# Regrouping the steps at the border of two mixture layers: each block's turn placed in steps of the other block

## The chip, the cores and the metric

The kernel runs on one core of a Trainium2 chip. The metric is the device time of one execution in microseconds (us), smaller being better. The core has five engines that run side by side, each through its own list of instructions in a fixed order: TensorE (PE in the rows, with PEld for its weight loads), VectorE (DVE), ScalarE (ACT), GpSimd (POOL) and SyncE (SP), which here issues the DMA transfers. An engine whose next instruction must wait holds back everything behind it in its list.

## The reference

Block attention gives a matrix x of 1536 rows and 512 columns, and two mixture-of-experts layers follow. The first has 4 experts and given weights, the second 8 experts and weights from a gate on its own input.

```python
def _moe_ref(x, domain_probs, w1, w2):          # first layer, E = 4
    p = domain_probs / (domain_probs.sum(-1, keepdims=True) + 1e-09)
    for e in range(E):
        h = np.maximum(x @ w1[e], 0.0)          # (1536, 1024)
        out += p[:, e:e + 1] * (h @ w2[e])      # (1536, 512)
...
def _moe2_ref(x, w_gate, w1, w2):               # second layer, E = 8
    logits = x @ w_gate
    P = np.exp(logits - logits.max())
    for _ in range(8):                          # rows, then columns
        P /= P.sum(1, keepdims=True) + 1e-09
        P /= P.sum(0, keepdims=True) + 1e-09
        P *= N / E
    for e in range(E):
        out += P[:, e:e + 1] * (np.maximum(x @ w1[e], 0.0) @ w2[e])
```

## The kernel before, in words

**Units, blocks, steps.** A unit is one expert's slice of 256 hidden columns: units 0 to 15 are the first layer, 16 to 47 the second. The rows of x are two blocks of 768. A step (u, b) is unit u on block b, 96 steps in all; before the change they go (0,0), (0,1), (1,0), (1,1) and so on.

**Two halves of a step.** Every fp32 factor is split into a high and a low part (names in hi and lo), and three matmuls stand for one. The first half of a step is seven products P1 to P7 of six matmuls each (`step_products`, L487), a fast block multiplication with seven products in place of eight. Its operands are sums and differences, made ahead for the weights (`w1_pieces`) and for x (`x_pieces`). P1, P3, P5 and P7 accumulate into one PSUM bank `px`, P2 and P6 into another (also named px in the rows), P4 into `pz`. Between them the bank must be read: ScalarE copies it after P1, P2 and P3 (c11 L521, c22 L526, c12 L530), VectorE adds it to c11 after P4, to c22 after P5, to c12 after P6 (L516). So P3 waits for the copy after P1, P5 for the copy after P3, and P7 for the addition to c22 after P5. ScalarE makes hhi from c by relu (L495) and VectorE makes hlo from both (L500). The second half is G: six tiles of six matmuls with w2 (`g2_tile`, L562 to L564), each followed by VectorE's accumulation into `acc` (L582). A step ordinarily runs its own seven products and then the G of the step before it.

**Weights.** SyncE loads w1 (L141) and w2 (L149) of a unit into `scr`, three buffers that serve in turn. ScalarE writes the high parts (L125), GpSimd the differences (L178) and the low parts (L128). `w1_pieces` and `w2_pieces` stand in the lists behind a step's products. Two sets of weights, a and b, alternate by unit.

**The turn.** When a block's first layer is done, its `acc` is transposed by TensorE (pxt, L592, eight groups of three), copied by ScalarE into two `scr` buffers (L596), and made into x operands. `x_pieces` has six rounds for each of two half-buffers, here r1 to r6: r1 casts 768 columns (ScalarE), low part by GpSimd; r2 casts 384 columns, low part by VectorE; r3 two subtractions on VectorE (L211); r4 casts their results, low part by GpSimd; r5 two more subtractions; r6 casts those, low part by VectorE. The gate (`gate_logits`: pg, gs, pl) and `sinkhorn` follow.

**Order.** `weave` takes a string, and each letter emits the next piece of one generator: P a product, G a tile, w a weight piece, T a turn piece, L a gate piece, s a piece of sinkhorn. This order is the order in every engine's list. At the border, block 0 is turned in step (15,1) by BND1 and BND2, and block 1 in step (16,0) by BND3 and BND4. In these two steps the products are followed by the step's own G.

Of the kernel before, what the change touches and what calls it, by code (L numbers as in the profile page):

```python
# [18 lines left out]
def local_global_attention_moe_moe(  # L19
# [13 lines left out]
    nc = tc.nc  # L33
# [162 lines left out]
    def w2_pieces(u, hi_eng, lo_eng):  # L196
        w = wsets[u % 2]
        s = stage[u, 2]
        for c in range(FC):
            yield split(w["w2hi"][:, c], w["w2lo"][:, c], s[:, c], hi_eng, lo_eng)  # L200
# [276 lines left out]
    def new_xf():  # L477
        return scratch(2, 2 * BLK)

    def product(u, b, a, x, pm, first=True):  # L480
        w = wsets[u % 2]
        n = 3 * KH
        i = 0
        for c in range(KH):
            xhi, xlo = xop[b, c]
            for l, r in (("w1hi", xhi), ("w1hi", xlo), ("w1lo", xhi)):
                nc.tensor.matmul(  # L487
                    pm, w[l][:, a, c, :], r[:, x, :],
                    start=first and i == 0, stop=i == n - 1, skip_group_check=True,
                )  # L490
                i += 1

    def relu_hi(u, b, f, t, c):
        hhi = hsets[(u * NB + b) % 2][0]
        nc.scalar.activation(out=hhi[:, f, t * HB:(t + 1) * HB], in_=c, func=AF.Relu)  # L495

    def relu_lo(u, b, f, t, c):
        hhi, hlo = hsets[(u * NB + b) % 2]
        sl = slice(t * HB, (t + 1) * HB)
        nc.vector.scalar_tensor_tensor(  # L500
            out=hlo[:, f, sl], in0=c, scalar=0.0, in1=hhi[:, f, sl].bitcast(F32),
            op0=ALU.max, op1=ALU.subtract,
        )

    def step_products(u, b):

        def temp(name):
            return xp.tile([P, HB], F32, name=name)  # L510

        def bank():
            return ps_x.tile([P, 512], F32, name="px", tag="x")[:, 0:HB]

        def add(c, pm):
            nc.vector.tensor_tensor(out=c, in0=pm, in1=c, op=ALU.add)  # L516

        px = bank()
        product(u, b, A11, B11, px)
        c11 = temp("c11")  # L520
        nc.scalar.copy(out=c11, in_=px)  # L521
        yield
        py = bank()
        product(u, b, S1, T1, py)
        c22 = temp("c22")
        nc.scalar.copy(out=c22, in_=py)  # L526
        yield
        product(u, b, S2, T2, px, False)
        c12 = temp("c12")
        nc.scalar.copy(out=c12, in_=px)  # L530
        yield
        pz = ps_m.tile([P, HB], F32, name="pz", tag="m")
        product(u, b, A12, B21, pz)
        add(c11, pz)
        relu_hi(u, b, 0, 0, c11)
        yield
        product(u, b, S3, T3, px, False)
        add(c22, px)
        relu_hi(u, b, 1, 1, c22)
        relu_lo(u, b, 0, 0, c11)  # L540
        yield
        product(u, b, S4, B22, py, False)
        add(c12, py)
        relu_hi(u, b, 0, 1, c12)
        relu_lo(u, b, 1, 1, c22)
        yield
        product(u, b, A22, T4, px, False)
        relu_hi(u, b, 1, 0, px)
        relu_lo(u, b, 0, 1, c12)
        relu_lo(u, b, 1, 0, px)  # L550
        yield

    raw, lg = set(), {}

    def g2_tile(u, b, t):
        layer, e, f = units[u]
        w = wsets[u % 2]
        hhi, hlo = hsets[(u * NB + b) % 2]
        pm = ps_m.tile([P, DM], F32, name="pm", tag="m")
        ts = slice(t * P, (t + 1) * P)  # L560
        for c in range(FC):
            nc.tensor.matmul(pm, hhi[:, c, ts], w["w2hi"][:, c, :], start=(c == 0), stop=False)  # L562
            nc.tensor.matmul(pm, hhi[:, c, ts], w["w2lo"][:, c, :], start=False, stop=False)  # L563
            nc.tensor.matmul(pm, hlo[:, c, ts], w["w2hi"][:, c, :], start=False, stop=(c == FC - 1))  # L564
        T = b * TPB + t
        first = e == 0 and f == 0
        if layer == 1 and "p" not in lg:
            assert e == 0
            raw.add(T)
            if first:  # L570
                nc.scalar.copy(out=acc[T], in_=pm)
            else:
                nc.vector.tensor_tensor(out=acc[T], in0=pm, in1=acc[T], op=ALU.add)
            return
        scal = (p1 if layer == 0 else pp)[:, T, e:e + 1]
        if T in raw:
            raw.remove(T)
            nc.vector.tensor_scalar_mul(acc[T], acc[T], pp[:, T, 0:1])
        if first:
            nc.vector.tensor_scalar_mul(acc[T], pm, scal)  # L580
        else:
            nc.vector.scalar_tensor_tensor(  # L582
                out=acc[T], in0=pm, scalar=scal, in1=acc[T], op0=ALU.mult, op1=ALU.add
            )
        if u == NU - 1:
            nc.sync.dma_start(out=out[T * P:(T + 1) * P, :], in_=acc[T])
# [11 lines left out]
    def turn_pieces(b):  # L598

        for c in range(KH):  # L600
            xfs[b, c] = new_xf()
            for th in range(2):
                for dh in range(2):
                    yield transpose_x(b, c, th, dh)
        los = (nc.gpsimd, nc.vector, nc.gpsimd, nc.vector)
        halves = [
            x_pieces(b, c, xfs[b, c], xfs[b, c], nc.scalar, los, nc.vector) for c in range(KH)
        ]
        for _ in range(6):
            for h in halves:  # L610
                yield next(h, None)

    def gate_logits(b):

# [57 lines left out]
        yield  # L672
        lg["p"] = pp

    def g2_tiles(u, b):
        for t in range(TPB):
            yield g2_tile(u, b, t)

    DONE = object()

# [8 lines left out]
    def head_of(gen, n):  # L689
        for _ in range(n):  # L690
            if next(gen, DONE) is DONE:
                return
            yield

    def chain(*gens):
        for g in gens:
            yield from g

    L = E1 * NFU - 1
    BND1, BN1 = "wwGGGGGGPTTTTPTPTTTPTPTPTPTTT", 15  # L700
    BND2 = "TGTGTGTGTGTG"
    BND3, BN3 = "PTPTTTPTPTTTPTPTPTTTT", 14
    BND4 = "TGTLGTLGTLGTLGTLGL"
    ENTRY = "GPwGPwGwPwGPwGPwGPwPww"
    STEADY = "PPPPPPPwGwGwGwGwwGwwG"
    LATE = "PsPsPsPsPsPsPwsGwsGwsGwwsGwwsGwsG"
    with tc.manual_schedule():
        early = chain(step_products(0, 0), g2_tiles(0, 0))
        side = {}

        def filler(w, n):
# [42 lines left out]
        with tc.tile_pool(name="attn", bufs=1) as apool:  # L754
# [13 lines left out]
        )  # L768
        weave(
            "PPwPwPwPwPwPw",  # L770
            P=step_products(0, 1),
            G=early,
            w=chain(
                w1_pieces(1, nc.vector, nc.gpsimd, nc.vector),
# [3 lines left out]
        load_w1(2)  # L778
        load_w2(2)

        def w_pieces(u, b):
            if u >= NU:
                return iter(())
            if b == 0:
                return w1_pieces(u, nc.scalar, nc.gpsimd, nc.gpsimd)
            return w2_pieces(u, nc.scalar, nc.gpsimd)

        for u in range(1, NU):
            for b in range(NB):
                prev = (u, 0) if b else (u - 1, 1)  # L790
                tiles = g2_tiles(*prev)
                prod = step_products(u, b)
                if (u, b) == (L, 1):
                    turn = turn_pieces(0)
                    weave(
                        BND1,
                        P=prod, G=tiles, T=head_of(turn, BN1), w=w_pieces(u + 1, 1),
                    )
                    weave(BND2, G=g2_tiles(u, 1), T=turn)
                elif (u, b) == (L + 1, 0):  # L800
                    turn = turn_pieces(1)
                    weave(BND3, P=prod, T=head_of(turn, BN3))
                    weave(BND4, G=g2_tiles(u, 0), L=gate_logits(0), T=turn)
                    load_w1(u + 1)
                    load_w2(u + 1)
                elif (u, b) == (L + 1, 1):
                    weave(
                        "wPLwPLwPLwPLwPLwPLwP", P=prod, L=gate_logits(1),
                        w=chain(w_pieces(u + 1, 0), w_pieces(u + 1, 1)),
                    )  # L810
                    load_w1(u + 2)
                    load_w2(u + 2)
                    sink = sinkhorn()
                else:
                    w = w_pieces(u + 1, b)
                    if u > L and "p" not in lg:
                        weave(
                            LATE, P=prod, G=tiles, w=w, s=head_of(sink, 12),
                        )
                    else:  # L820
                        order = ENTRY if (u, b) == (1, 0) else STEADY
                        weave(order, P=prod, G=tiles, w=w)
                    if u + 2 < NU and (u, b) != (L, 0):
                        (load_w2 if b else load_w1)(u + 2)
        for _ in g2_tiles(NU - 1, 1):
            pass


# [26 lines left out]
```

## Time and profile before

| what | value |
|---|---|
| time, median of 3 runs | 1644.41 us (1643.33 to 1644.82) |
| time of the profiled execution | 1645.07 us |
| its span, first to last instruction | 1643.4 us |
| TensorE busy | 1599.0 us, 97% of the span |
| VectorE, ScalarE, GpSimd busy | 56%, 36%, 34% |
| mean granted TensorE clock | 0.990 |
| stretch of the border, 600 to 664.56 us | TensorE busy 58.40 of 64.56 us |

Busy time is the time in which an engine ran an instruction; a matmul's row is longer than the distance to the next one's start, because matmuls overlap. The granted clock is 1.00 at 2.4 GHz and 0.50 at 1.2 GHz. What an engine waited for is told in brackets, with the instruction that released it.

### The profile page before, as it was taken

The numbers are of one execution on the slowest core, as the hardware profiler recorded it, in microseconds if no ns is written. First come the engines' busy times: TensorE is split into PE (matmuls) and PEld (weight loads), VectorE is DVE, ScalarE is ACT, GpSimd is POOL, SyncE is SP. The second block draws the span as 40 slices with busy tenths as digits, with TensorE's granted clock in tenths as the row PEclk, the third lists the DMA queues.
The fourth block names the chain that finished last, engine by engine and source line by source line (L and its number), as shares of the span: only waits on it lengthen the run. The fifth ranks groups of instructions, "written<-read, shape, count | busy, mean of one in ns | idle before, by whom it ended". The sixth has DMA issues, their size and how long they took to land.

```text
span 1643.4 us, 21876 instructions
## 1 busy us (share of the span) xinstructions
PE 1599.0 (97%) x8419; PEld 1437.7 (87%) x8419; DVE 922.3 (56%) x1711; ACT 586.5 (36%) x1369; POOL 558.3 (34%) x642
## 2 busy tenths in 40 slices
PE   6879999999999999999999999999999999999999
PEld 5768899899899987889998998998998999989987
DVE  6886554554554556675555555545545545555555
ACT  4763233333333335433333333323323323323321
POOL 3644333323324333424324324324323323333330
PEclk9889999999999999999999999999999999999999
DMA  9831001001001100101100100100100100100102
GB/s 185 161 83 52 26 26 52 27 26 50 28 26 40 38 1 26 53 26 41 37 27 31 47 26 27 52 26 27 52 27 27 51 26 26 52 26 26 52 0 78
DMA packets 84520, 70.26 MB, mean 43 GB/s; under 512 B 36032, under 2 KB 69056, under 8 KB 84416
## 3 DMA queue, kind: packets, MB, share of 16 engines
q1 hardware_dynamic: 84416, 68.87, 14.5%
q8 instruction: 66, 1.08, 0.3%
q14 instruction: 38, 0.31, 0.1%
HBM read 64.53 MB, written 3.15 MB: 41 GB/s over the span
## 4 chain that ended last, share of the span: by engine, by line
PE 90%; DVE 6%; ACT 1%; issue 1%; DMA 1%; POOL 0%; SPq 0%; DVEq 0%; ACTq 0%
PE px L487 35%; PE pm L564 16%; PE pm L563 16%; PE pm L562 16%; PE pz L487 6%; ACT s L398 1%; DVE scr L211 1%; DVE vr L342 1%; DVE s L388 1%; DVE sm L402 1%; PE pg L622 0%; DVE hlo_b L500 0%; DVE c L516 0%; DMA vn<-in_v_dram 0%; DMA scr<-in_moe_w_dram 0%
## 5 line engine op out<-in xcount | busy, mean ns | idle before, releaser
L582 DVE SCALAR_TENSOR_TENSOR acc<-pm,pp,acc 128x512 f32<-128x512 f32 x359 | 269.6, 751 | 195.0 <-PE pm L564 193.3
L516 DVE TENSOR_TENSOR c<-pz,c 128x384 f32<-128x384 f32 x96 | 53.4, 557 | 317.9 <-PE pz L487 317.8
L128 POOL TENSOR_TENSOR w1lo_b<-scr,w1hi_b 128x512 fp32r<-128x512 f32 (+1 forms) x144 | 116.9, 830 | 317.0 <-ACT w1hi_b L125 309.4
L128 POOL TENSOR_TENSOR w1lo_a<-scr,w1hi_a 128x512 fp32r<-128x512 f32 (+1 forms) x144 | 118.4, 841 | 305.9 <-ACT w1hi_a L125 296.0
L521 ACT COPY c<-px 128x384 f32<-128x384 f32 x96 | 46.1, 480 | 436.6 <-PE px L487 436.5
L487 PE MATMUL px<-xhi,w1hi_a 128*128 128x384 f32 x576 | 195.5, 339 | 2.0 <-ACT c L521 1.0
L487 PE MATMUL px<-xhi,w1hi_b 128*128 128x384 f32 x576 | 194.1, 337 | 0.8 <-ACT c L530 0.8
L487 PE MATMUL px<-xlo,w1hi_a 128*128 128x384 f32 x576 | 193.8, 336 | 0.2 <-POOL xlo L128 0.2
L487 PE MATMUL px<-xhi,w1lo_a 128*128 128x384 f32 x576 | 193.8, 336 | 0.0
L487 PE MATMUL px<-xhi,w1lo_b 128*128 128x384 f32 x576 | 193.3, 336 | 0.0
L487 PE MATMUL px<-xlo,w1hi_b 128*128 128x384 f32 x576 | 193.3, 336 | 0.0
L582 DVE SCALAR_TENSOR_TENSOR acc<-pm,p,acc 128x512 f32<-128x512 f32 x180 | 135.0, 751 | 97.0 <-PE pm L564 97.0
L178 POOL TENSOR_TENSOR scr<-scr 128x256 f32<-128x256 f32 x188 | 137.6, 742 | 3.7
L516 DVE TENSOR_TENSOR c<-px,c 128x384 f32<-128x384 f32 x192 | 107.0, 557 | 46.6 <-PE px L487 46.5
L128 POOL TENSOR_TENSOR w2lo_a<-scr,w2hi_a 128x512 fp32r<-128x512 f32 x48 | 61.2, 1296 | 161.8 <-ACT w2hi_a L125 159.1
L128 POOL TENSOR_TENSOR w2lo_b<-scr,w2hi_b 128x512 fp32r<-128x512 f32 x48 | 60.9, 1292 | 161.0 <-ACT w2hi_b L125 161.0
L564 PE MATMUL pm<-w2hi_b,hlo_b 128*128 128x512 f32 x288 | 113.4, 394 | 2.3 <-DVE hlo_b L500 2.3
L495 ACT ACTIVATE hhi_a<-c 128x384 fp32r<-128x384 f32 x144 | 75.6, 525 | 112.0 <-DVE c L516 112.0
L562 PE MATMUL pm<-w2hi_b,hhi_b 128*128 128x512 f32 x288 | 112.8, 391 | 0.5 <-ACT hhi_b L495 0.5
L562 PE MATMUL pm<-w2hi_a,hhi_a 128*128 128x512 f32 x288 | 112.5, 391 | 0.7 <-ACT hhi_a L495 0.7
L564 PE MATMUL pm<-w2hi_a,hlo_a 128*128 128x512 f32 x288 | 112.6, 391 | 0.5 <-DVE hlo_a L500 0.5
L495 ACT ACTIVATE hhi_b<-c 128x384 fp32r<-128x384 f32 x144 | 75.6, 525 | 104.6 <-DVE c L516 104.5
(148 smaller groups left out, 3613.0 us busy)
## 6 DMA issues: line engine op xcount, KB each, us to landing
scr<-in_moe_w_dram SPq DMA_DIRECT2D x96, 512.0 KB, 4.6
vs<-in_v_dram SPq DMA_DIRECT2D x16, 240.0 KB, 4.8
kn<-in_k_dram SPq DMA_DIRECT2D x16, 192.0 KB, 4.0
qn<-in_q_dram SPq DMA_DIRECT2D x16, 192.0 KB, 4.4
vn<-in_v_dram SPq DMA_DIRECT2D x8, 384.0 KB, 3.8
out_dram<-acc SPq DMA_DIRECT2D x12, 256.0 KB, 2.0
vs<-vb SPq DMA_DIRECT2D x8, 144.0 KB
vs<-in_v_dram SPq DMA_DIRECT2D x32, 24.0 KB, 4.5
```

Source lines behind the costliest of these rows:

```text
L128: lo_eng.tensor_tensor(out=lo, in0=src, in1=hi.bitcast(F32), op=ALU.subtract)
L178: sum_eng.tensor_tensor(out=st[:, o], in0=x, in1=y, op=op)
L211: sum_eng.tensor_tensor(out=out, in0=x, in1=y, op=ALU.subtract)
L342: nc.vector.tensor_reduce(out=vr[i], in_=vn[i].rearrange("x h c d -> x h d c"), axis=AX.X, op=ALU.add)
L487: nc.tensor.matmul(pm, w[l][:, a, c, :], r[:, x, :], start=first and i == 0, stop=i == n - 1, skip_group_check=True,)
L495: nc.scalar.activation(out=hhi[:, f, t * HB:(t + 1) * HB], in_=c, func=AF.Relu)
L516: nc.vector.tensor_tensor(out=c, in0=pm, in1=c, op=ALU.add)
L521: nc.scalar.copy(out=c11, in_=px)
L562: nc.tensor.matmul(pm, hhi[:, c, ts], w["w2hi"][:, c, :], start=(c == 0), stop=False)
L563: nc.tensor.matmul(pm, hhi[:, c, ts], w["w2lo"][:, c, :], start=False, stop=False)
L564: nc.tensor.matmul(pm, hlo[:, c, ts], w["w2hi"][:, c, :], start=False, stop=(c == FC - 1))
L582: nc.vector.scalar_tensor_tensor(out=acc[T], in0=pm, scalar=scal, in1=acc[T], op0=ALU.mult, op1=ALU.add)
```

## The change

Steps are now listed by number n in `steps`. Units 14 and 15 go as (14,0), (15,0), (14,1), (15,1), and units 16 and 17 as (16,0), (17,0), (16,1), (17,1); all other pairs keep their order. Block 0 is turned during (14,1) and (15,1), block 1 during (16,0) and (17,0), by the strings TURN1 and TURN2. The gate of block 0 stands in (16,1) and that of block 1 in (17,1) (GATE). Every step runs the G of the step before it, at the border too. The w1 pieces of a unit stand in the step just ahead of its first, its w2 pieces in its first step; before, they stood one unit earlier. `sinkhorn` begins at (18,0) in place of (17,0).

```diff
-        for u in range(1, NU):
-            for b in range(NB):
-                prev = (u, 0) if b else (u - 1, 1)
...
-    BND1, BN1 = "wwGGGGGGPTTTTPTPTTTPTPTPTPTTT", 15
-    BND2 = "TGTGTGTGTGTG"
-    BND3, BN3 = "PTPTTTPTPTTTPTPTPTTTT", 14
-    BND4 = "TGTLGTLGTLGTLGTLGL"
-    ENTRY = "GPwGPwGwPwGPwGPwGPwPww"
+        order += (a, c, x, y) if u in (L - 1, L + 1) else (a, x, c, y)
+    steps = [(u, b, n) for n, (u, b) in enumerate(order)]
...
+    w1_in = {first[u] - 1: u for u in range(2, NU)}
+    w2_in = {first[u]: u for u in range(2, NU)}
...
+        loads.setdefault(first[u] - 2, []).append((load_w1, u))
...
+        loads.setdefault(first[u] - 1, []).append((load_w2, u))
...
+    ENTRY = "GPGPGPwGwPGPwGPwGPwPww"
     STEADY = "PPPPPPPwGwGwGwGwwGwwG"
     LATE = "PsPsPsPsPsPsPwsGwsGwsGwwsGwwsGwsG"
+    TURN1 = "PPwGwGwGwGwGwGwwwwPTTPTTPTTPTTPT"
+    TURN2 = "PTPTPTPTPTPwPwGwGwGwGwGwGwww"
+    GATE = "PLPLPLPLPLPLPLGwLGwLGwLGwLGwG"
...
         for _ in range(6):
             for h in halves:
-                yield next(h, None)
+                next(h, None)
+            yield
...
+            if S[0:2] in ((L - 1, 1), (L + 1, 0)):
+                turn = turn_pieces(0 if S[1] else 1)
+                more, letters = {"T": head_of(turn, TURN1.count("T"))}, TURN1
+            elif S[0:2] in ((L, 1), (L + 2, 0)):
+                more, letters = {"T": turn}, TURN2
```

VectorE's list in step (15,1) before: c11, c22 and c12 are the three additions, xlo00 and xlo01 the low parts of block 0's two halves, and the rows at L211 are the subtractions of r3.

```order
L516 TENSOR_TENSOR c11_5365<-pz_5426,c11_5365 128x384
L516 TENSOR_TENSOR c22_5395<-px_5358,c22_5395 128x384
L500 SCALAR_TENSOR_TENSOR hlo_b_1609<-c11_5365,hhi_b_1608 128x384
L516 TENSOR_TENSOR c12_5409<-px_5388,c12_5409 128x384
L500 SCALAR_TENSOR_TENSOR hlo_b_1609<-c22_5395,hhi_b_1608 128x384
L128 TENSOR_TENSOR xlo00_82<-scr_5367,xhi00_81 128x384
L500 SCALAR_TENSOR_TENSOR hlo_b_1609<-c12_5409,hhi_b_1608 128x384
```

The same engine in step (15,1) of the changed kernel (its lines are numbered one or two higher), with r2, r3, r5 and r6 in order.

```order
L128 TENSOR_TENSOR xlo00_82<-scr_5249,xhi00_81 128x384
L128 TENSOR_TENSOR xlo01_84<-scr_5250,xhi01_83 128x384
L211 TENSOR_TENSOR scr_5249<-scr_5249 128x384 x2
L211 TENSOR_TENSOR scr_5250<-scr_5250 128x384 x2
L517 TENSOR_TENSOR c11_5340<-pz_5371,c11_5340 128x384
L211 TENSOR_TENSOR scr_5249<-scr_5249 128x384 x2
L211 TENSOR_TENSOR scr_5250<-scr_5250 128x384 x2
L517 TENSOR_TENSOR c22_5353<-px_5333,c22_5353 128x384
L501 SCALAR_TENSOR_TENSOR hlo_b_1609<-c11_5340,hhi_b_1608 128x384
L128 TENSOR_TENSOR xlo00_82<-scr_5249,xhi00_81 128x768
L128 TENSOR_TENSOR xlo01_84<-scr_5250,xhi01_83 128x768
L517 TENSOR_TENSOR c12_5365<-px_5346,c12_5365 128x384
```

Before, the three additions stood ahead of all subtractions; now two low parts and eight subtractions stand ahead of the addition to c22.

ScalarE's list in the same step of the changed kernel, from the last relu of the step before to the cast of r4: xhi00 and xhi01 are the casts, px_5333 and px_5346 the two banks of (15,1).

```order
L496 ACTIVATE hhi_a_97<-px_5175 128x384
L125 CAST xhi00_81<-scr_5249 128x768
L125 CAST xhi01_83<-scr_5250 128x768
L522 COPY c11_5340<-px_5333 128x384
L125 CAST xhi00_81<-scr_5249 128x384
L125 CAST xhi01_83<-scr_5250 128x384
L527 COPY c22_5353<-px_5346 128x384
L531 COPY c12_5365<-px_5333 128x384
L125 CAST xhi00_81<-scr_5249 128x768
```

Before, the step's first copy c11 stood ahead of all casts of the turn; now two casts of 768 columns stand between the last relu and that copy.

## Rows read from the trace of the kernel before

**Rows 1.** Stretches, TensorE alone: length, busy time and instructions, granted clock, DMA share, GB/s.
```profile
398.09:406.25 8.16, 8.16 (x37) 1.00 0.01 2
406.25:413.58 7.33, 7.33 (x43) 1.00 0.41 143
600.00:664.56 64.56, 58.40 (x315) 0.97 0.07 22
114.35:120.18 5.83, 5.77 (x46) 0.51 0.01 3
615.16:618.31 3.15, 3.15 (x7) 0.50 0.00 0
```

**Rows 2.** What TensorE waited for, whole span: us in total, times, longest.
```profile
PE pm L564 <- DVE hlo_b L500: 2.3, 1, 2.3
...
PE pl L634 <- ACT gs L628: 1.2, 2, 0.6
...
PE pxt L592 <- DVE acc L582: 0.9, 2, 0.5
PE px L487 <- ACT c L530: 0.8, 1, 0.8
PE pm L562 <- ACT hhi_a L495: 0.7, 1, 0.7
PE pm L562 <- ACT hhi_b L495: 0.5, 1, 0.5
PE pm L564 <- DVE hlo_a L500: 0.5, 1, 0.5
```

**Rows 3.** Timeline of TensorE in a step of sinkhorn: P6's last matmul, P7's first.
```profile
703.57 0.34 PE L487 MATMUL px<-xhi,w1lo_a 128*128 128x384 f32 x1
704.80 0.45 PE L487 MATMUL px<-xhi,w1hi_a 128*128 128x384 f32 x1 [0.89 <-DVE c L516]
```

**Rows 4.** Timeline of an ordinary step with w1 pieces, ScalarE: start us, us, instruction.
```profile
404.80 1.11 ACT L125 CAST w1hi_a<-scr 128x256 fp32r<-128x256 f32 x3 [1.93 <-POOL scr L178]
```

**Rows 5.** Timeline of the same step and the next, GpSimd.
```profile
399.33 1.29 POOL L128 TENSOR_TENSOR w1lo_a<-scr,w1hi_a 128x512 fp32r<-128x512 f32 x1 [13.00 <-ACT w1hi_a L125]
...
405.43 2.13 POOL L128 TENSOR_TENSOR w1lo_a<-scr,w1hi_a 128x256 fp32r<-128x256 f32 x3
414.86 2.54 POOL L128 TENSOR_TENSOR w2lo_a<-scr,w2hi_a 128x512 fp32r<-128x512 f32 x2 [7.30 <-ACT w2hi_a L125]
```

**Rows 6.** Timeline of ScalarE early on: a cast of x and the copy behind it.
```profile
132.44 0.83 ACT L125 CAST xhi<-scr 128x768 fp32r<-128x768 f32 x1 [2.40 <-DVE scr L211]
133.18 0.47 ACT L521 COPY c<-px 128x384 f32<-128x384 f32 x1
```

**Rows 7.** Timeline of the turn of block 0, VectorE.
```profile
612.00 2.17 DVE L128 TENSOR_TENSOR xlo<-scr,xhi 128x384 fp32r<-128x384 f32 x1
...
615.49 2.34 DVE L211 TENSOR_TENSOR scr<-scr 128x384 f32<-128x384 f32 x4
617.75 0.75 DVE L582 SCALAR_TENSOR_TENSOR acc<-pm,p,acc 128x512 f32<-128x512 f32 x1
618.41 3.65 DVE L211 TENSOR_TENSOR scr<-scr 128x384 f32<-128x384 f32 x2
...
622.64 1.01 DVE L211 TENSOR_TENSOR scr<-scr 128x384 f32<-128x384 f32 x2
624.24 0.94 DVE L128 TENSOR_TENSOR xlo<-scr,xhi 128x768 fp32r<-128x768 f32 x1
```

**Rows 8.** The same stretch, GpSimd.
```profile
609.81 3.94 POOL L128 TENSOR_TENSOR xlo<-scr,xhi 128x768 fp32r<-128x768 f32 x2 [13.37 <-ACT xhi L125]
617.64 4.00 POOL L128 TENSOR_TENSOR xlo<-scr,xhi 128x768 fp32r<-128x768 f32 x2 [3.89 <-ACT xhi L125]
```

**Rows 9.** Timeline of TensorE: four groups of transposes in a row.
```profile
601.84 1.47 PE L592 MATMUL pxt<-ident,acc 128*128 128x128 f32 x12
```

**Rows 10.** DMA of 620 to 700 us: weight loads, KB each, median us to landing.
```profile
scr<-in_moe_w_dram SPq DMA_DIRECT2D x6, 512.0 KB, 3.5
```

More of the change, by code (lines that the diff above doesn't have):

```diff
@@ L478, in new_xf, with product @@
         return scratch(2, 2 * BLK)
-    def product(u, b, a, x, pm, first=True):
+    def product(S, a, x, pm, first=True):
+        u, b, n_ = S
         w = wsets[u % 2]
@@ L491, in product, with relu_hi, relu_lo @@
                 i += 1
-    def relu_hi(u, b, f, t, c):
-        hhi = hsets[(u * NB + b) % 2][0]
+    def relu_hi(S, f, t, c):
+        hhi = hsets[S[2] % 2][0]
         nc.scalar.activation(out=hhi[:, f, t * HB:(t + 1) * HB], in_=c, func=AF.Relu)
-    def relu_lo(u, b, f, t, c):
-        hhi, hlo = hsets[(u * NB + b) % 2]
+    def relu_lo(S, f, t, c):
+        hhi, hlo = hsets[S[2] % 2]
         sl = slice(t * HB, (t + 1) * HB)
@@ L503, in relu_lo, with step_products @@
         )
-    def step_products(u, b):
+    def step_products(S):
         def temp(name):
@@ L518, in step_products @@
         px = bank()
-        product(u, b, A11, B11, px)
+        product(S, A11, B11, px)
         c11 = temp("c11")
@@ L523, in step_products @@
         py = bank()
-        product(u, b, S1, T1, py)
+        product(S, S1, T1, py)
         c22 = temp("c22")
@@ L527, in step_products @@
         yield
-        product(u, b, S2, T2, px, False)
+        product(S, S2, T2, px, False)
         c12 = temp("c12")
@@ L532, in step_products, with g2_tile @@
         pz = ps_m.tile([P, HB], F32, name="pz", tag="m")
-        product(u, b, A12, B21, pz)
+        product(S, A12, B21, pz)
         add(c11, pz)
-        relu_hi(u, b, 0, 0, c11)
+        relu_hi(S, 0, 0, c11)
         yield
-        product(u, b, S3, T3, px, False)
+        product(S, S3, T3, px, False)
         add(c22, px)
-        relu_hi(u, b, 1, 1, c22)
-        relu_lo(u, b, 0, 0, c11)
+        relu_hi(S, 1, 1, c22)
+        relu_lo(S, 0, 0, c11)
         yield
-        product(u, b, S4, B22, py, False)
+        product(S, S4, B22, py, False)
         add(c12, py)
-        relu_hi(u, b, 0, 1, c12)
-        relu_lo(u, b, 1, 1, c22)
+        relu_hi(S, 0, 1, c12)
+        relu_lo(S, 1, 1, c22)
         yield
[L547 to L550, printed above, removed]
+        product(S, A22, T4, px, False)
+        relu_hi(S, 1, 0, px)
+        relu_lo(S, 0, 1, c12)
+        relu_lo(S, 1, 0, px)
         yield
     raw, lg = set(), {}
-    def g2_tile(u, b, t):
+    def g2_tile(S, t):
+        u, b, n_ = S
         layer, e, f = units[u]
         w = wsets[u % 2]
-        hhi, hlo = hsets[(u * NB + b) % 2]
+        hhi, hlo = hsets[n_ % 2]
         pm = ps_m.tile([P, DM], F32, name="pm", tag="m")
@@ L601, in turn_pieces @@
             xfs[b, c] = new_xf()
-            for th in range(2):
+        for th in range(2):
+            for c in range(KH):
                 for dh in range(2):
@@ L673, in sinkhorn, with g2_tiles @@
         lg["p"] = pp
-    def g2_tiles(u, b):
+    def g2_tiles(S):
         for t in range(TPB):
-            yield g2_tile(u, b, t)
+            yield g2_tile(S, t)
     DONE = object()
@@ L699, in local_global_attention_moe_moe, with w_pieces @@
     L = E1 * NFU - 1
-    BND1, BN1 = "wwGGGGGGPTTTTPTPTTTPTPTPTPTTT", 15
-    BND2 = "TGTGTGTGTGTG"
-    BND3, BN3 = "PTPTTTPTPTTTPTPTPTTTT", 14
-    BND4 = "TGTLGTLGTLGTLGTLGL"
-    ENTRY = "GPwGPwGwPwGPwGPwGPwPww"
+    order = []
+    for u in range(0, NU, 2):
+        a, c = (u, 0), (u + 1, 0)
+        x, y = (u, 1), (u + 1, 1)
+        order += (a, c, x, y) if u in (L - 1, L + 1) else (a, x, c, y)
+    steps = [(u, b, n) for n, (u, b) in enumerate(order)]
+    at = {(u, b): n for u, b, n in steps}
+    first = [at[u, 0] for u in range(NU)]
+    w1_in = {first[u] - 1: u for u in range(2, NU)}
+    w2_in = {first[u]: u for u in range(2, NU)}
+    loads = {}
+    for u in range(3, NU):
+        loads.setdefault(first[u] - 2, []).append((load_w1, u))
+    for u in range(3, NU):
+        loads.setdefault(first[u] - 1, []).append((load_w2, u))
+    def w_pieces(n):
+        if n in w2_in:
+            yield from w2_pieces(w2_in[n], nc.scalar, nc.gpsimd)
+        if n in w1_in:
+            yield from w1_pieces(w1_in[n], nc.scalar, nc.gpsimd, nc.gpsimd)
+    ENTRY = "GPGPGPwGwPGPwGPwGPwPww"
     STEADY = "PPPPPPPwGwGwGwGwwGwwG"
     LATE = "PsPsPsPsPsPsPwsGwsGwsGwwsGwwsGwsG"
+    TURN1 = "PPwGwGwGwGwGwGwwwwPTTPTTPTTPTTPT"
+    TURN2 = "PTPTPTPTPTPwPwGwGwGwGwGwGwww"
+    GATE = "PLPLPLPLPLPLPLGwLGwLGwLGwLGwG"
     with tc.manual_schedule():
-        early = chain(step_products(0, 0), g2_tiles(0, 0))
+        early = chain(step_products(steps[0]), g2_tiles(steps[0]))
         side = {}
@@ L770, in local_global_attention_moe_moe @@
             "PPwPwPwPwPwPw",
-            P=step_products(0, 1),
+            P=step_products(steps[1]),
             G=early,
@@ L779, in local_global_attention_moe_moe @@
         load_w2(2)
[L781 to L786, printed above, removed]
-        for u in range(1, NU):
-            for b in range(NB):
-                prev = (u, 0) if b else (u - 1, 1)
[L791 to L824, printed above, removed]
@@ L825, in local_global_attention_moe_moe @@
-        for _ in g2_tiles(NU - 1, 1):
+        sink = None
+        for n in range(2, len(steps)):
+            S = steps[n]
+            more, letters = {}, STEADY
+            if S[0:2] in ((L - 1, 1), (L + 1, 0)):
[3 more added lines that the diff above has]
+                more, letters = {"T": turn}, TURN2
+            elif S[0:2] in ((L + 1, 1), (L + 2, 1)):
+                more, letters = {"L": gate_logits(S[0] - L - 1)}, GATE
+                sink = sinkhorn()
+            elif S[0] > L and "p" not in lg:
+                more, letters = {"s": head_of(sink, LATE.count("s"))}, LATE
+            elif n == 2:
+                letters = ENTRY
+            weave(
+                letters, P=step_products(S), G=g2_tiles(steps[n - 1]), w=w_pieces(n), **more
+            )
+            for load, u in loads.get(n, ()):
+                load(u)
@@ L826, in local_global_attention_moe_moe @@
+        for _ in g2_tiles(steps[-1]):
             pass
```

## The prediction

> **What bounds the kernel now.** I read the stretches of an ordinary step first. Its G takes 8.16 us and its seven products 7.33 us [rows 1]. TensorE is busy throughout, so a product is 1.05 us, a G tile 1.36 us, a step 15.5 us, and no other engine's work shows in the time. What can be gained is what TensorE waits for. The list of its waits [rows 2] puts seven groups at places that the change touches. Behind the products of (15,1) its own G waits for hhi (0.5 us) and hlo (2.3). Behind those of (16,0) it waits for the same two (0.7 and 0.5). The transposes wait for acc (0.9, two waits), the gate for gs (1.2, two waits), and in step (1,0) a product waits for c12 (0.8). That makes 6.9 us in nine waits. The border's stretch agrees: 64.56 − 58.40 = 6.2 us idle [rows 1], all but the 0.8 that lies in (1,0). Next I read the clock. After the 2.3 us wait seven matmuls take 3.15 us at a granted clock of 0.50, the 1.2 GHz level [rows 1]; at 8.16/36 = 0.227 us each they would take 1.59 us, so 1.6 us more are lost.
>
> **What the change removes.** In the new order the G of a step always stands behind the next step's products, or, in TURN1, behind two of them. Hence the four waits for hhi and hlo go, and with them the slow clock behind the longest. The transposes come one product after the last accumulation, and the gate's gs gets a product or a tile as cover. In (1,0) no weight piece stands in ScalarE's list any longer. A wait costs a little more than its idle time: in the row of P7 0.89 us are shown idle, while 704.80 − 703.57 − 0.17 = 1.06 us are lost [rows 3]. Nine times about 0.2 is 1.7 us. Gain: 6.9 + 1.6 + 1.7 = 10.2 us. Its lower end is the idle time and the clock, 8.5.
>
> **The steady steps cost nothing.** w1 pieces now stand in the step just ahead of their use. In an ordinary step they end at 405.43 + 2.13 = 407.56 [rows 5], 1.3 us into the next products, whose first began at 406.25 [rows 1]. The parts are needed in order, the last by P6, 5.2 us in. ScalarE is through with its casts at 404.80 + 1.11 = 405.91 [rows 4], and P1 ends at 407.3, so the copy c11 isn't held. The w2 pieces have a whole step. If that cover were gone, the late part would be a wait of P2 or P5, once per unit.
>
> **Step (15,0): 0.6 us.** The step ahead now carries w2 and w1 pieces together. GpSimd starts 1.24 us after G begins (399.33 − 398.09), spends 2.54 on w2 [rows 5], and ScalarE's last cast ends 405.91 − 399.33 = 6.58 after w1's first low part [rows 4, 5]. This makes 10.4, the copy c11 behind it 10.8; P3 wants it at 8.16 + 2.09 = 10.25. Bounds 0 and 1.
>
> **Steps (15,1) and (17,0): the turn inside the products.** This term decides. I count from the start of P1.
> - ScalarE's last relu of the step before begins at about 0.2 and takes 0.5; then come the two r1 casts, 133.18 − 132.44 = 0.74 apart [rows 6]. So the copy c11 runs from 2.1 to 2.6. P3, due at 2.1, is 0.5 late, and P6 ends at 2.6 + 4 × 1.05 = 6.8.
> - GpSimd's two r1 low parts start behind the first cast, at 1.5, and take 3.94 [rows 8]: 5.45.
> - VectorE's two r2 low parts start at 3. One gets in between GpSimd's two, the other ends behind the second: the row at 612.00 took 2.17 us and ended 0.4 after GpSimd did (614.17 against 609.81 + 3.94) [rows 7, 8]. That is 5.9.
> - r3: four subtractions 2.34, to 8.1. GpSimd starts r4 2.15 after r3 starts (617.64 − 615.49), at 7.95.
> - The addition to c11, then r5. Its first two subtractions took 3.65 beside r4's low parts and ended 4.42 after GpSimd's start (622.06 − 617.64) [rows 7, 8]: 12.4. The other two take 1.01: 13.3. The addition to c22 follows, 13.9.
> - P7 must not write the bank before that addition has read it. Rows 3 show this very wait. P7 starts at 13.9 in place of 6.8: **7.1 us idle**, and the G of the step before stands behind it in TensorE's list.
>
> The clock falls in such a wait. Lost after it: 1.6 by the stretch after 2.3 us idle; half of 5.83, 2.9, by the stretch after an early wait of 4 us [rows 1]. I take 2.0, nearer to the first, since the same kind of matmul follows. Each of the two steps costs 0.5 + 7.1 + 2.0 = 9.6 us, together 19.2.
>
> Is the hold of VectorE by GpSimd real? Four subtractions alone take 2.34, two beside GpSimd 3.65, while an accumulation from PSUM beside it takes 0.75 [rows 7]. Had they 0.58 each throughout, r3 would still wait for r1's low parts (to 6.0), and r5 would end at 8.9 and the addition at 9.45. P7 would wait 2.65. The rows say hold, so I keep 7.1, with 2.65 as the other end. The Trainium skill (SBUF — State Buffer, Who interferes with whom) states it as a rule that speaks against this change: a VectorE instruction with two SBUF inputs contends with a GpSimd instruction that reads SBUF, and the loser blocks for the whole instruction. By that rule the wait of P7 is the 7.1 us; without it, the 2.65.
>
> **Step (16,0): 1.0 us.** The load of w2(16) takes the scr buffer of w1(16), which GpSimd leaves late: behind the addition to c22 come the relu, r6 (two casts, two low parts at 0.94 [rows 7]), the addition to c12, a relu and a cast, to 18.6; the last reading comes 405.43 + 1.42 − 399.33 = 7.5 later [rows 5], at 26.1, and landing takes 3.5 [rows 10]: 29.6. P1 of (16,0) starts at 13.9 + 1.05 + 8.16 + 2.0 = 25.1, so the data are there 4.5 into the step. ScalarE holds the casts of w2 and w1 ahead of the copy c12: 4.5 + 0.7 + 2.54 + 6.58 + 0.5 = 14.8. P5 would be due at 2.09 + 8.16 + 2 × 1.05 + 4 × 0.37 (a group of transposes [rows 9]) = 13.8. Bounds 0 and 3.5, the latter with a slow clock behind it.
>
> **Sum.** 0.6 + 19.2 + 1.0 − 10.2 = +10.6 us. The profiled execution took 1645.07, of which the span is all but 1.7; it becomes 1655.7. The median of the runs is 0.7 lower, so I forecast **1655.0**.
>
> **The rivals.**
> - *Vector work isn't held by GpSimd* in this mixture. For it: the accumulation at 0.75. Against: both rows with two SBUF inputs. Each turn costs 0.5 + 2.65 + 1.6 = 4.75: 0.6 + 9.5 + 1.0 − 10.2 = +0.9, 1645.3, no change. Chance 0.08.
> - *P7 doesn't wait* (other side): VectorE has added to c22 by the time P6 ends, since the turn's chain runs ahead under cover of the step's earlier products. The price is then 0.6 + 1.0 + 2 × 0.5 − 10.2 = −7.6, 1636.8. It decides for faster where the two waits with their clock stay under 4.3 us together, 2.1 each. For it: the order gives each round one product of distance, and the G behind was always ready. Against: r1 to r5 is 13 us of dependent work and a product 1.05. Chance 0.08.
> - *Worse:* the clock takes 2.9 after each (+1.8), w2(16) comes late (+4.1 with its clock), and a low part of r2 misses its gap (+0.5 each turn): 1661.9. Chance 0.09.
>
> The forecast has 0.75.
>
> **Range and chances.** From 1646, which leaves out the first two rivals, to 1662, which takes in the third. A measurement tells about 0.2%, 3.3 us, from no change. Slower by more: the forecast and the third rival, 0.84; within: the first, 0.08; faster: the second, 0.08.
>
> **What will show it.** Right: two waits of `px` for VectorE's c of about 7 us in (15,1) and (17,0); the row of two subtractions near 3.7 us beside r4; a granted clock of 0.50 behind both; the waits of rows 2 at hhi, hlo, gs and pxt gone; about 1 us at c12 in (16,0), 0.6 at c11 in (15,0). Wrong: P7 following P6 at once, a turn's eight subtractions near 4.7 us in all, or waits for w1's parts at the head of ordinary steps.

## The result, and the profile after

The changed kernel takes 1653.38 us (median of 4 runs, 1652.39 to 1655.11) where the kernel before took 1644.62 beside it (4 runs, 1643.33 to 1645.38): a ratio of 1.0055, with a 95% interval of 1.0038 to 1.0073. The forecast was 1655.0, with a range of 1646 to 1662. The changed kernel ran once more beside the later experiments: 1654.32 us (6 runs), a ratio of 1.0059 (1.0047 to 1.0071).

The list of TensorE's waits in the changed kernel, from 540 to 760 us (us in total, times, longest), answers to [rows 2]:

```profile
PE px L488 <- DVE c L517: 14.3, 3, 6.7
PE px L488 <- ACT c L522: 1.1, 3, 0.4
PE px L488 <- ACT c L531: 0.8, 1, 0.8
```

The eight waits of [rows 2] in this stretch (hlo, hhi, gs and the acc of the transposes) are gone, and the ninth, for c12 in (1,0), too. In their place stand two of 6.7 us for an addition to c. The third in that line is the 0.9 us in a step of sinkhorn, which both kernels have [rows 3].

The timeline of TensorE (start, length, instruction, idle time before it and what ended that) shows where: P3 of (15,0), P3 of (15,1), the last matmul of P6 and the first of P7 in (15,1), P5 of (16,0), and P3 and P7 of (17,0).

```profile
561.02 0.44 PE L488 MATMUL px<-xhi,w1hi_b 128*128 128x384 f32 x1 [0.33 <-ACT c L522]
595.40 0.44 PE L488 MATMUL px<-xhi,w1hi_b 128*128 128x384 f32 x1 [0.40 <-ACT c L522]
599.52 0.34 PE L488 MATMUL px<-xhi,w1lo_b 128*128 128x384 f32 x1
606.57 0.69 PE L488 MATMUL px<-xhi,w1hi_b 128*128 128x384 f32 x1 [6.72 <-DVE c L517]
632.26 0.44 PE L488 MATMUL px<-xhi,w1hi_a 128*128 128x384 f32 x1 [0.85 <-ACT c L531]
639.46 0.44 PE L488 MATMUL px<-xhi,w1hi_b 128*128 128x384 f32 x1 [0.40 <-ACT c L522]
650.62 0.69 PE L488 MATMUL px<-xhi,w1hi_b 128*128 128x384 f32 x1 [6.72 <-DVE c L517]
```

The windows behind the two long waits (length, TensorE busy and its instructions, granted clock, DMA share, GB/s): both run at the 1.2 GHz level.

```profile
606.57:609.94 3.37, 3.37 (x10) 0.50 0.02 5
650.62:654.42 3.80, 3.80 (x11) 0.50 0.05 16
```

What held the addition is read from VectorE's timeline in (15,1), and from GpSimd's beside it: r2's low parts, r3, the addition to c11, r5, the addition to c22; then r1's and r4's low parts.

```profile
595.79 2.90 DVE L128 TENSOR_TENSOR xlo<-scr,xhi 128x384 fp32r<-128x384 f32 x2 [1.69 <-ACT xhi L125]
598.61 2.34 DVE L211 TENSOR_TENSOR scr<-scr 128x384 f32<-128x384 f32 x4
600.87 0.55 DVE L517 TENSOR_TENSOR c<-pz,c 128x384 f32<-128x384 f32 x1
601.34 4.71 DVE L211 TENSOR_TENSOR scr<-scr 128x384 f32<-128x384 f32 x4
605.97 0.55 DVE L517 TENSOR_TENSOR c<-px,c 128x384 f32<-128x384 f32 x1
```
```profile
594.31 3.96 POOL L128 TENSOR_TENSOR xlo<-scr,xhi 128x768 fp32r<-128x768 f32 x2 [24.12 <-ACT xhi L125]
600.76 3.93 POOL L128 TENSOR_TENSOR xlo<-scr,xhi 128x768 fp32r<-128x768 f32 x2 [2.49 <-ACT xhi L125]
```

The same four subtractions take 2.34 us in r3 and 4.71 in r5; r5 has GpSimd at work beside it, r3 only in its last 0.2 us. The addition to c22 waits its turn until 605.97, though P5 ended some 7 us earlier, and P7 follows it.

**Comparing profiles.** One execution's span also holds the attention, which is the same code in all kernels here and yet ends up to 5 us apart from profile to profile. So I measure from the third accumulation of (0,0) (start of its row) to the last matmul of the program. For the kernel before and the changed one, two rows each:

```profile
127.36 0.75 DVE L580 TENSOR_SCALAR acc<-pm,p 128x512 f32<-128x512 f32 x1 [0.46 <-PE pm L564]
...
1639.18 0.39 PE L564 MATMUL pm<-w2hi_b,hlo_b 128*128 128x512 f32 x1
```
```profile
125.51 0.75 DVE L582 TENSOR_SCALAR acc<-pm,p 128x512 f32<-128x512 f32 x1 [0.44 <-PE pm L566]
...
1646.77 0.39 PE L566 MATMUL pm<-w2hi_b,hlo_b 128*128 128x512 f32 x1
```

That is 1511.82 and 1521.26 us, a loss of 9.4, beside 8.8 between the medians. The table below has this distance for every kernel, as "from (0,0)".

### The profile page after: what moved, and what is told of

It reads as the page before. It is cut to its first block, busy times and chain, and to the rows that moved or that the text cites. A ratio compares the mean times of both kernels' runs of the same rounds, so it can differ in the third digit from the quotient of the medians.

```text
span 1650.9 us, 21887 instructions
## 1 busy us (share of the span) xinstructions
PE 1599.4 (97%) x8419; PEld 1438.0 (87%) x8419; DVE 920.6 (56%) x1711; ACT 586.8 (36%) x1369; POOL 558.0 (34%) x642
## 4 chain that ended last, share of the span: by engine, by line
PE 88%; DVE 5%; ACT 2%; POOL 2%; issue 2%; DMA 1%; SPq 0%; DVEq 0%; POOLq 0%; ACTq 0%
PE px L488 34%; PE pm L565 15%; PE pm L566 15%; PE pm L564 15%; PE pz L488 6%; DVE scr L211 1%; ACT s L398 1%; DVE vr L342 1%; POOL scr L178 1%; POOL w1lo_a L128 1%; PE ps L379 1%; DVE xlo L128 0%; DVE sm L402 0%; DVE c L517 0%; PE pg L626 0%
## 5 line engine op out<-in xcount | busy, mean ns | idle before, releaser
L584 DVE SCALAR_TENSOR_TENSOR acc<-pm,pp,acc 128x512 f32<-128x512 f32 x347 | 260.3, 751 | 186.5 <-PE pm L566 185.2
L488 PEld LDWEIGHTS px<-xhi,w1hi_b 128*128 128x128 f32 x576 | 108.6, 189 | 19.5 <-DVE c L517 15.3
L564 PE MATMUL pm<-w2hi_a,hhi_a 128*128 128x512 f32 x312 | 122.4, 392 | 0.0
L566 PE MATMUL pm<-w2hi_a,hlo_a 128*128 128x512 f32 x312 | 122.4, 392 | 0.0
L565 PE MATMUL pm<-w2lo_a,hhi_a 128*128 128x512 f32 x312 | 122.3, 392 | 0.0
L565 PE MATMUL pm<-w2lo_b,hhi_b 128*128 128x512 f32 x312 | 121.8, 391 | 0.0
L566 PE MATMUL pm<-w2hi_b,hlo_b 128*128 128x512 f32 x312 | 121.8, 390 | 0.0
L564 PE MATMUL pm<-w2hi_b,hhi_b 128*128 128x512 f32 x312 | 121.6, 390 | 0.0
```

The costliest lines, as they stand in the source:

```text
L488: nc.tensor.matmul(pm, w[l][:, a, c, :], r[:, x, :], start=first and i == 0, stop=i == n - 1, skip_group_check=True,)
L584: nc.vector.scalar_tensor_tensor(out=acc[T], in0=pm, scalar=scal, in1=acc[T], op0=ALU.mult, op1=ALU.add)
```

## The experiments

Two sets, each on one chip beside the kernel before. In the first set that kernel took 1642.46 us (9 runs), in the second 1644.51 (22 runs). "Against changed" is the difference from 1521.26; the row in brackets is the changed kernel's repeat.

| kernel | median, us | ratio to before, 95% | from (0,0), us | against changed |
|---|---|---|---|---|
| x1: r4's low parts on VectorE | 1650.20 | 1.0025 to 1.0051 | 1517.87 | −3.4 |
| x2: r5, r6 behind P7 | 1648.78 | 1.0020 to 1.0046 | 1514.61 | −6.7 |
| x3: w1 pieces ahead of w2 pieces | 1653.08 | 1.0048 to 1.0073 | 1519.54 | −1.7 |
| x4: turn without r1 to r6 | 1633.54 | 0.9927 to 0.9955 | 1501.73 | −19.5 |
| (changed kernel again) | 1654.32 | 1.0047 to 1.0071 | 1521.99 | +0.7 |
| x5: x2 and x3, own buffer for the sums | 1643.29 | 0.9983 to 1.0001 | 1510.09 | −11.2 |
| x6: x5, turn spread by its due times | 1641.74 | 0.9975 to 0.9993 | 1509.94 | −11.3 |
| x7: x6, all low parts on VectorE | 1639.18 | 0.9956 to 0.9980 | 1505.70 | −15.6 |

**x1. Is r5 long because GpSimd works beside it?** r4's low parts go to VectorE, behind the addition to c22.

```diff
-        los = (nc.gpsimd, nc.vector, nc.gpsimd, nc.vector)
+        los = (nc.gpsimd, nc.vector, nc.vector, nc.vector)
...
+        if late:
+            yield nc.scalar.copy(out=hi[:, T1:T3], in_=tx[:, :, HB:BLK])
...
+        if late:
+            los[2].tensor_tensor(
+                out=lo[:, T1:T3], in0=tx[:, :, HB:BLK], in1=hi[:, T1:T3].bitcast(F32),
+                op=ALU.subtract,
+            )
```

> In each turn the two low parts of r4 are computed by VectorE in place of GpSimd, at the place of r6, behind the addition to c22. So no GpSimd instruction runs while VectorE makes the subtractions of r5. Theory (GpSimd holds VectorE): r5's four subtractions take 2.3 us as r3's did, in place of the 4.7 us from the first's start to the last's end; the wait of P7 for the addition to c22 falls from 6.7 to about 4.4 us in (15,1) and in (17,0), and the time by 4 to 5 us, to about 1649. Rival (r5 is long by its own kind, or waits for ScalarE): r5 stays at 4.7 us, the waits at 6.7, the time within 1 us of the changed kernel's.

VectorE's timeline in (15,1) of x1, with r3, the addition to c11, r5, the addition to c22; and P7 behind it:

```profile
599.47 2.34 DVE L211 TENSOR_TENSOR scr<-scr 128x384 f32<-128x384 f32 x4
601.73 0.55 DVE L525 TENSOR_TENSOR c<-pz,c 128x384 f32<-128x384 f32 x1
602.20 1.95 DVE L211 TENSOR_TENSOR scr<-scr 128x384 f32<-128x384 f32 x4
604.07 0.55 DVE L525 TENSOR_TENSOR c<-px,c 128x384 f32<-128x384 f32 x1
```
```profile
604.67 0.69 PE L496 MATMUL px<-xhi,w1hi_b 128*128 128x384 f32 x1 [3.94 <-DVE c L525]
...
631.33 0.61 PE L496 MATMUL px<-xhi,w1hi_a 128*128 128x384 f32 x1 [2.12 <-ACT c L539]
...
648.52 0.69 PE L496 MATMUL px<-xhi,w1hi_b 128*128 128x384 f32 x1 [3.96 <-DVE c L525]
```

With GpSimd idle, the same r5 takes 1.95 us in place of 4.71, and both waits of P7 fall by 2.8. The hold is real, and the rival falls in both its forms: r5 isn't long by its own kind, and r4's casts, which are still on ScalarE here, don't make it long. The gain was over-expected: the distance from (0,0) fell by 3.4 where 4 to 5 were forecast, since the wait for c12 in (16,0) grew from 0.85 to 2.12, with a slow clock behind it. Counted from the third accumulation of (0,0), which lies 1.03 later in this profile, the copy c11 of (16,0) is 3.1 us earlier than in the changed kernel (616.75 against 618.84), but the load of w2(16), which waits for r6 and w1(16), only 2.0 (617.82 against 618.83).

**x2. Does P7 wait because r5 is listed ahead of the addition?**

```diff
-    TURN2 = "PTPTPTPTPTPwPwGwGwGwGwGwGwww"
+    TURN2 = "PTPTPTPPPPTTwGwGwGwGwGwGwww"
```

The string also moves the turn step's first two weight pieces behind P7.

> In the second step of each turn, r5 and r6 stand behind P7 and its addition; r1 to r4 stay between P1 and P5. Theory (P7 waits because VectorE's list has r5 ahead of the addition to c22): the wait falls from 6.7 to about 2.3 us, what r1 to r3 take; the low clock behind it is shorter or gone. Given back: the sixth G tile waits about 1.2 us for an accumulation behind r5, and w1(16), whose sums need the buffers that r6 frees, comes about 1.4 us late for (16,0). Sum about -5, to about 1648.5. Rival (the bank of P7 is late for another cause, the addition itself or ScalarE): the wait stays within 1 us of 6.7 and the time that of the changed kernel.

TensorE's waits in x2, 540 to 760 us:

```profile
PE px L488 <- DVE c L517: 5.0, 3, 2.1
PE px L488 <- ACT c L531: 3.6, 1, 3.6
PE px L488 <- ACT c L522: 1.1, 3, 0.4
```

P7's two waits fall to 2.1 each (the line has sinkhorn's 0.9 as well), what r1 to r3 take. So most of the wait in the changed kernel came from r5 standing ahead of the addition, as the theory has it. The two things to be given back came out otherwise: no G tile waited, and (16,0) waited 3.6 us for c12, where w1(16) was expected to come about 1.4 us late. Here too the load of w2(16) is late (619.52), and ScalarE's casts of w2(16) stand ahead of the copy c12.

**x3. Is the lateness of (15,0) and (16,0) the order of the weight pieces?**

```diff
-        if n in w2_in:
-            yield from w2_pieces(w2_in[n], nc.scalar, nc.gpsimd)
         if n in w1_in:
             yield from w1_pieces(w1_in[n], nc.scalar, nc.gpsimd, nc.gpsimd)
+        if n in w2_in:
+            yield from w2_pieces(w2_in[n], nc.scalar, nc.gpsimd)
```

> In every step that carries both, the w1 pieces are emitted ahead of the w2 pieces. Theory (the lateness of (15,0) and (16,0) is the lists of ScalarE and GpSimd, with w2 ahead of w1): the wait of 0.33 us for c11 in (15,0) and that of 0.85 us for c12 in (16,0) go, about -1.7 us with their restarts, to about 1651.7. Rival (the copy c12 of (16,0) is late through the load of w2(16) alone): the 0.33 goes, the 0.85 stays or grows, and the time changes by less than 0.6 us.

TensorE's waits in x3, 540 to 760 us:

```profile
PE px L488 <- DVE c L517: 14.3, 3, 6.7
PE px L488 <- ACT c L522: 0.8, 2, 0.4
```

In x3 the wait of 0.33 us at P3 of (15,0) and that of 0.85 at P5 of (16,0) are both gone, and that is what it shows. The distance from (0,0) falls by 1.7, as expected, but this fit isn't evidence: the two profiles of the changed kernel differ by 0.7 between themselves, the slow clock behind P7 lasted 3.3 and 5.0 us here in place of 3.4 and 3.8, and the medians can't tell so little.

**x4. What does the regrouping give without the turn inside the products?**

```diff
         for _ in range(6):
-            for h in halves:
-                next(h, None)
             yield
```

> This kernel leaves out the six rounds r1 to r6 of both turns, so the second layer multiplies the first layer's x operands; the transposes stay. Theory (the turn inside the products is the whole loss of the change, about 2 x 9.2 us, and 0.6 and 1.2 us at (15,0) and (16,0) come from weights): the two waits of 6.7 us and the slow clock behind them go, and the time falls by about 18 us, to about 1635, which lies under the kernel before by the 9 to 10 us that the regrouping itself gives. Rival (the regrouping gives less than 10 us, and something else in it costs): the time stays over 1640.

TensorE's waits in x4, 540 to 760 us:

```profile
PE px L488 <- DVE c L517: 0.9, 1, 0.9
PE px L488 <- ACT c L522: 0.3, 1, 0.3
```

Sinkhorn's wait is left, and that of (15,0). The 19.5 us are the turn inside the products, with what it makes late in (16,0). Against the kernel before x4 is 10.1 us shorter (1511.82 − 1501.73); with the 0.5 that (15,0) still loses, the regrouping itself gives 10.6, in a kernel that has nothing to do in the place of the six rounds.

**The changed kernel again,** in the rounds of the next three.

> The changed kernel itself once more, in the same rounds as the three below, so that they can be read against it as well as against the kernel before. Expected: 9 us over the kernel before, as measured; two waits of 6.7 us at P7.

Its time, its two waits of 6.7 us and its distance from (0,0) came out as before, but for a longer slow clock behind P7 (the rows are in the last section) and no wait for c12 in (16,0), since P5 of that step is due later there.

**x5. Sums of w1 in a buffer of their own.** x2 and x3 together, and `st`, the buffer of the sums, no longer one of the three `scr`; the load of w1(16) goes one step earlier.

```diff
-        st = scratch(4, KD * FU).rearrange("x a (c f) -> x a c f", c=KH)
+        if u >= 2:
+            st = wb.tile([P, 4, KD * FU // 4], F32, name="st", bufs=1)
...
-        loads.setdefault(first[u] - 2, []).append((load_w1, u))
+        loads.setdefault(first[u] - (3 if u == L + 1 else 2), []).append((load_w1, u))
```

> r5 and r6 behind P7, w1 pieces ahead of w2 pieces, and in addition a buffer of their own (4 KB a partition, free after the attention) for the sums of w1, with the load of w1(16) one step earlier. Theory (the longer wait for c12 in (16,0), 3.6 us and a low clock behind it, came from w1(16), whose sums wait for a buffer that r6 frees, and from w2(16), whose load waits for that): it goes with the sums in a buffer of their own, while P7 keeps its two waits of about 2.1 us; the time is 5 us under that of the run with r5 and r6 behind P7 alone, about 1643 to 1645, level with the kernel before. Rival (the c12 copy is late through ScalarE's casts of the turn or the copies of pxt): a wait for c12 of over 1 us stays in (16,0), and the time is at 1647 or more.

The wait for c12 is gone and P7 keeps its two of 2.1, as expected; small ones are left at P3 of the turn steps (0.4 each), for a low part of w1(16) (0.6) and for an acc (0.5). Which of the three things added to x2 removed the wait isn't shown: the order of x3 alone removed the 0.85 us of the changed kernel, and neither the buffer nor the earlier load ran without it. The time is within 0.2% of the kernel before.

**x6 and x7. The turn spread by its due times, and without GpSimd.** The transposes stand right behind the G tiles, r1 and r2 in the step before, r3 behind P1, r4 behind P5, r5 behind P6, r6 behind the first G tile. Below are the two strings that x6 and x7 share, and then the one line in which x7 differs from x6:

```diff
+    TURN1 = "PPwGwGwGwGwGwGwwwwTTPTTPTTPTTPTPT"
+    TURN2 = "PTPPPPTPTPwGTwGwGwGwGwGww"
...
-        los = (nc.gpsimd, nc.vector, nc.gpsimd, nc.vector)
+        los = (nc.vector, nc.vector, nc.vector, nc.vector)
```

> As the run with the buffer of its own, but the transposes stand right behind the G tiles and r1, r2 in the step before, so that the second step of a turn has r3 behind P1, r4 behind P5, r5 behind P6 and r6 behind the first G tile; low parts of r1 and r4 still on GpSimd. Theory (GpSimd's low parts hold VectorE): r2 and r3 are held by r1's low parts, and P7 waits still about 1 us in each turn; r5 takes 4.7 us beside r4's low parts and the accumulations behind it make G wait 1 to 3 us; together 2 to 4 us over the run below. Rival (no hold): equal to the run below within 1 us.

> As the run above, but all low parts of the turn are computed by VectorE. Theory: nothing holds VectorE before P7, its list has 1.9, 0.9 and 2.3 us of r1 to r3 ahead of the addition to c22 and all behind it hides under G: waits of P7 of at most 0.5 us, no low clock, and the time is the changed kernel's less 16 to 18, 1634 to 1637, which beats the kernel before by 7 to 10. Rival (VectorE becomes the bound: 11 us for the turn, 4.5 for six accumulations, 3.5 for hlo and the additions in 15.5 us): G or the next products wait 2 to 5 us in each turn, and the time is 1640 or more.

TensorE's waits from 540 to 760 us in x6, then in x7:

```profile
PE px L492 <- DVE c L521: 2.7, 3, 0.9
PE pm L568 <- DVE acc L588: 2.4, 1, 2.4
PE px L492 <- ACT c L526: 2.2, 2, 1.1
```
```profile
PE px L492 <- ACT c L526: 2.2, 2, 1.1
PE px L492 <- DVE c L521: 0.9, 1, 0.9
PE px L492 <- ACT w1hi_a L125: 0.6, 1, 0.6
PE px L492 <- POOL w1lo_a L128: 0.6, 1, 0.6
```

In x6 P7 waits 0.9 us in each turn, and G 2.4 us for an acc behind r5, after which the granted clock is 0.50 for some 3 us. In x7 all of this is gone; P7 follows P6 within 0.2 us of its due time, and the clock stays at 1.00 from 540 to 760 us. x6 is 2.6 us over x7 by the medians and 4.2 by the distance, where 2 to 4 were forecast, so its rival (no hold, equal within 1 us) falls. x7 (5 runs) is faster than the kernel before by 0.20 to 0.44%. Of the kernels that leave nothing out it is the only one that is faster by the 0.2% that the prediction counted as a difference, and at the near end of the interval only just. It missed its forecast of 1634 to 1637 by 2 us: each turn still makes P3 wait 1.1 us, and w1(16) is late by two waits of 0.6. In ScalarE's list the casts of r2 (0.91 us for the two) now stand ahead of the copy c11 as well as those of r1, which fits the longer wait of P3 (1.1 in place of 0.4); no run moves them back. VectorE did not become the bound.

## Why the prediction was right

**The gain: right.** 10.2 us were forecast; x4 measures 10.6. All nine waits went, and no ordinary step waits for its weights. The forecast's restarts were rounded up: nine times the 0.17 us of its own row is 1.5, which makes 10.0.

**P7 in (15,1) and (17,0): right by its steps.** I counted 7.1 us; from the last matmul of P6 6.88 are lost (606.57 − 599.52 − 0.17, by the rows above). The count can be laid over the rows, with P1 starting at 592.75. r2 was to begin at 3 and end at 5.9, that is at 595.75 and 598.65: it runs from 595.79 to 598.69. GpSimd was to start r4 2.15 us behind r3's start: 600.76 − 598.61 = 2.15. r5 was to have its first two subtractions done at 12.4 and all four at 13.3, which is 4.7 after its start; it took 4.71, the first two 3.77 where the row of before had 3.65. The Trainium skill (SBUF — State Buffer, Who interferes with whom), which has the loser of such a contention blocked for the whole instruction, spoke against the change and gave the same 7.1. The runs agree: r5, with two inputs in SBUF, takes 4.71 us beside GpSimd and 1.95 without it, while the addition at 600.87, which has one input in PSUM, takes 0.55 with GpSimd at work.

**The clock: right in kind, a little too high in size.** 2.0 us were taken for each turn. In the first window behind P7 its six matmuls and three of G start, the tenth in the row at its end. By [rows 1] they take 6 × 0.174 + 3 × 0.227 = 1.73 us at full clock, in place of 3.37; in (17,0) six and four take 1.95 in place of 3.80. So 1.6 and 1.9 are lost. The repeat lost 2.6 behind each wait (last section). The 2.0 was a choice between 1.6 and 2.9, and no row of before could decide it; that it lies so near is in part luck.

**The small terms: right.** (15,0): 0.33 us idle, 0.5 lost with the restart, against 0.6. P3 of (15,1) and of (17,0): 0.40 idle, 0.6 with the restart, against 0.5. (16,0): 0.85 idle, 1.06 with the restart, against 1.0, by the very chain that was counted: the load of w2(16) leaves late, and ScalarE keeps the casts of w2 and w1 ahead of c12, as x3 bears out, where the w1 casts go first and the wait is gone.

**The sum.** +10.6 was forecast, 9.4 measured over the distance from (0,0): the gain was 0.4 larger, the two waits of P7 0.4 and the clock 0.5 smaller, P3 0.2 larger and (15,0) 0.1 smaller, which makes 9.4. With the repeat's clock the same sum would come out 1.7 us higher, so the last digit of this agreement means little. None of the rivals came: no-hold is ruled out by x1; "P7 doesn't wait" held only in x7, whose turn is laid out for it; and of the three terms of "worse" only the clock moved its way, with the 2.6 of the repeat against 2.9.

## What to carry to other kernels

Moving a chain of dependent work under another step's cover helps only if no instruction of that step that TensorE waits for stands behind it in an engine's list: the eight subtractions themselves were harmless (x7 has them all), but ahead of an addition due one product later they, and the rounds that they wait for, cost 6.7 us in each turn. A list of dependent rounds is best laid out by when each result is due, with the bank-freeing instruction ahead of it, and GpSimd was no second pair of hands here: giving its low parts to VectorE made the kernel faster (x6 to x7). And price a reordering by both sides: here the regrouping was worth 10.6 us, and the layout of the turn decided whether it showed.

## What the runs showed of the hardware

**The hold passes from one to the other, an instruction at a time.** In x6 GpSimd's list goes on behind r4 without a gap, and r5's four subtractions took 6.92 us, the longest here. VectorE's rows (the first subtraction alone, the last alone, all four), then GpSimd's:

```profile
603.58 2.21 DVE L215 TENSOR_TENSOR scr<-scr 128x384 f32<-128x384 f32 x1
...
609.41 1.09 DVE L215 TENSOR_TENSOR scr<-scr 128x384 f32<-128x384 f32 x1
...
603.58 6.92 DVE L215 TENSOR_TENSOR scr<-scr 128x384 f32<-128x384 f32 x4
```
```profile
603.41 4.09 POOL L128 TENSOR_TENSOR xlo<-scr,xhi 128x768 fp32r<-128x768 f32 x2 [4.97 <-ACT xhi L125]
607.46 1.61 POOL L128 TENSOR_TENSOR w1lo_a<-scr,w1hi_a 128x512 fp32r<-128x512 f32 x1
609.04 1.05 POOL L182 TENSOR_TENSOR st<-scr 128x256 f32<-128x256 f32 x1
```

Four subtractions pass while four GpSimd instructions do: each lasts about as long as the GpSimd instruction beside it, 2.21 us beside a low part of 768 columns, 1.09 beside a sum of 256. So in these rows the price of the hold goes by the size of the other engine's instructions, not by one's own 0.5 us. That GpSimd is held too is seen in x7, where a low part of w1 of 512 columns, beside the end of r5 and two hlo, took 2.44 us against 1.29 [rows 5]:

```profile
609.31 2.44 POOL L128 TENSOR_TENSOR w1lo_a<-scr,w1hi_a 128x512 fp32r<-128x512 f32 x1 [35.47 <-ACT w1hi_a L125]
```

**The slow clock does not follow the wait alone.** Behind waits of the same 6.7 us it lasted 3.4 and 3.8 us in the one profile of the changed kernel and 5.5 in both turns of the other:

```profile
607.57:613.05 5.48, 5.48 (x14) 0.50 0.18 59
651.70:657.19 5.49, 5.49 (x14) 0.50 0.30 97
```

At full clock these fourteen matmuls (six of P7, eight of G) take 2.86 us by [rows 1], so 2.6 are lost each time. Behind P7's wait of 2.1 us it came in (15,1) of x2 but not in (17,0); in x5 it was the other way round. The windows behind these four waits in x2, then in x5:

```profile
605.46:608.82 3.36, 3.36 (x10) 0.51 0.00 0
648.12:651.50 3.38, 3.38 (x16) 1.00 0.00 0
```
```profile
603.38:606.70 3.32, 3.32 (x16) 1.00 0.02 5
642.96:646.27 3.31, 3.31 (x10) 0.50 0.00 0
```

What decides between the two stays open; by these profiles a sum for this kernel should carry 0 to 1.5 us behind a wait of 2 us, and 1.6 to 2.6 behind one of 6.7.
